# Early routing over 25 tiles with shorter last lags, and the next routing's compares behind the list in the experts

## The chip, the cores and the metric

The kernel runs on one core of a Trainium2 chip. The metric is the device time of one launch in microseconds (us); the times given are medians over runs. Engines are named as in the profile: PE is TensorE's matmul, PEld its weight load, DVE is VectorE, ACT is ScalarE, POOL is GpSimd, SP is SyncE, which issues most of the transfers.

## What is computed

Attention over 8 batches and 8 heads (S = 576 positions, D = 64), whose output, 4608 tokens of 512 numbers, goes through a mixture of 8 experts. Each token is given to one expert, each expert takes at most 576 tokens, and the pairs are handed out in the order of all logits from the largest down.

```python
def _attn_ref(q, k, v):                       # factor = 4, scale = 1 / sqrt(D)
    q_d = q.reshape(B, H, Sd, factor, D).mean(axis=3)      # k_d, v_d likewise
    out_up = np.repeat(sm_attn(q_d, k_d, v_d), factor, axis=2)
    mask = np.abs(pos[:, None] - pos[None, :]) < factor
    scores = np.where(mask, scale * np.matmul(q, k.transpose(0, 1, 3, 2)), -1000000000.0)
    ...
    return out_up + np.matmul(softmax(scores), v)

def _moe_ref(x, w_gate, w1, w2):
    logits = x @ w_gate                       # 4608 x 8
    order = np.argsort(-logits.flatten())
    for idx in order:
        tok, e = int(idx) // E, int(idx) % E
        if assigned[tok] >= 0 or counts[e] >= cap:         # cap = 576
            continue
        assigned[tok] = e
        counts[e] += 1
    for e in range(E):
        h = np.maximum(x[assigned == e] @ w1[e], 0.0)
        out[assigned == e] = h @ w2[e]
```

## The kernel before

**Attention.** The 4608 tokens are 36 tiles of 128 (index u), 4.5 to a batch. A tile goes through stages, each with a lag in the table LOC, counted in tiles: s0 and s1 (loc_s) make the scores of the band on PE, DVE takes their maximum (L541) and subtracts it (L542), ACT the exponential (L544); t (loc_t) transposes the result on PE (L552), and ACT copies it out as pt (L563); v0 and v1 (loc_v) multiply with v (L574), and norm divides by the sums on DVE (L450, L451, L453), which gives x. Then "add" (log_a) adds the downsampled attention's rows (L582, on POOL from the middle of the program), "st" stores x, "lt" (log_t) transposes x on PE (L592), ACT makes the high half of xt (L601) and DVE the low half (L602), and "lm" (log_m) makes the logits: four products with the high half (L617), four with the low half (L620), and a sum on DVE (L622) into lg.

The downsampled attention of a batch (down: scores, transposes of sd at L391 and L396, products with vd at L407 to L420) lies between these, spread from tile time DWS[b][0] to DWS[b][1] after the batch's first tile (DW where a batch has no entry). The transposes of q and k (L327) lie there too.

The order is written by hand: each step has a time in tiles (u + its lag), all steps are sorted by it, and each engine runs its instructions in that order. PE's steps are counted as pieces; "after(n, f)" puts f behind the n-th piece that follows, so FT is how many pieces behind the transposes the low half stands. From tile UE on, lags over 2 are shortened by the share CE for each tile. VWT is how far ahead of a tile its v is loaded. The loads and stores are issued by SP in the same order.

**Routing.** A logit becomes a key of two 16-bit halves, xh and xl (setup, L930 to L990). A search over the threshold that 576 tokens reach compares the keys with 64 thresholds at a time (compare, L822, into level[0] and level[1]) and counts the ones on PE (count, L855); three levels follow one another for xh and three for xl. Then rank (L909, L910) numbers the chosen tokens, the list turns the numbers into an index: ohh and ohl are one-hot rows of the high and low bits (L1099, L1112), r holds the rows of tokens (L1102, L1106), 18 products (L1115) add them up, and idx goes to the gathers. The counts, the rank, the list and the "sums" of totals (L898) share two PSUM buffers named pR in turn. The logits, setup and first level of tiles that are done are taken care of during attention: SETUP = {27: 0, 35: 28} starts setup over tiles 0 to 27 behind the logits of tile 27, and over 28 to 35 behind those of tile 35; SPACE is the distance of its steps in tiles. "ready" and "rest" prepare and finish the tables.

**Experts.** One expert after another: 576 tokens in 5 chunks, 312 products of xt with w1 (pH, L1258) and of ht with w2 (pX, L1299), each split into high and low halves. While expert i runs, the routing for expert i + 1 runs on DVE with its small products put between the big ones on PE: in the first stage after the products that TURN and BEHIND name, later by "place", which puts each group of routing products behind the last product whose planned time in the stage is not later than its entry in PACE (PACES for one stage). The last two of its 17 entries are those of the list and the sums. On DVE the instructions stand as the scheduler places them by their estimated times; a NoSync dependency ("behind_") makes one stand behind another.

## Time and profile before

| | |
|---|---|
| median of 3 runs | 720.87 us (719.96 to 724.84) |
| the profiled execution's own time | 722.95 us |
| its span | 721.3 us |
| mean granted clock of PE | 0.959 |
| PE busy | 648.9 us, 90% |
| DVE busy | 543.9 us, 75% |
| ACT busy | 338.2 us, 47% |
| POOL busy | 233.2 us, 32% |

The span is what the profile's times count from; the execution's own time has 1.65 us around it. The shares are means over pieces of different kind: attention until about 258 us, the last logits and the first routing until 298 us, eight experts of about 51 us each behind it. So the rows below are taken by stretches. In the rows "start, us" are the start and duration in microseconds; "out<-in" are the program's names without their numbers; the brackets at the end hold how long the engine had stood idle just before, and what it waited for.

### The profile page before, as it was taken

Reading aid. Unit: us, or ns where it says so; the run is one execution under the profiler, and the core shown is the slowest. Engines: PE = TensorE matmul, PEld = TensorE weight load, DVE = VectorE, ACT = ScalarE, POOL = GpSimd, SP = SyncE. Lnnn points to the kernel's source line nnn. Section 1 sums busy time; section 2 is a strip of 40 time slices with the busy share of each in tenths; the row PEclk is TensorE's granted clock in tenths of the full one; section 3 lists DMA queues with packets and bytes.
Section 4 is the critical chain, followed back from the end, with each engine's and each line's share of the span. In section 5 each row is a group of like instructions: output and inputs, shape, how many; then the busy total and the mean of one; then the engine's idle time right before and its main releaser. Section 6 shows DMA issues by size and latency. Waiting matters only on the chain.

```text
span 721.3 us, 21912 instructions
## 1 busy us (share of the span) xinstructions
PE 648.9 (90%) x8895; PEld 447.8 (62%) x8895; DVE 543.9 (75%) x1599; ACT 338.2 (47%) x649; POOL 233.2 (32%) x305
## 2 busy tenths in 40 slices
PE   7788999989899942899999899999999999999994
PEld 4566778777777731575575475574674674765841
DVE  5688989988989887887899698797797886533500
ACT  4448777787786520542442443443343324434410
POOL 4773565635737240401502402203103106202011
PEclk9799999999999965899999999999999999999997
DMA  9956779687985631704506817627647359806001
GB/s 261 230 149 192 223 191 232 191 216 197 230 220 155 177 112 48 251 2 166 200 1 252 172 25 265 151 82 231 120 149 195 90 202 212 317 21 111 2 30 37
DMA packets 132156, 113.71 MB, mean 158 GB/s; under 512 B 81240, under 2 KB 109912, under 8 KB 132056
## 3 DMA queue, kind: packets, MB, share of 16 engines
q1 hardware_dynamic: 124760, 90.76, 45.2%
q0 software_dynamic: 6432, 20.98, 9.5%
q8 instruction: 70, 1.15, 0.7%
q10 hardware_dynamic: 864, 0.58, 0.3%
q14 instruction: 30, 0.25, 0.1%
HBM read 85.74 MB, written 19.46 MB: 146 GB/s over the span
## 4 chain that ended last, share of the span: by engine, by line
PE 29%; DVE 20%; issue 15%; POOL 4%; DMA 3%; ACT 2%; POOLq 0%; SPq 0%; DVEq 0%; ACTq 0%
PE pX L1299 11%; PE pH L1258 10%; DVE level L822 2%; DVE wl L1182 2%; DVE ht L1285 2%; POOL xg L1197 2%; PE pR L855 2%; POOL out_dram L1309 2%; DMA xg<-x_dram,idx 1%; DVE x L453 1%; DVE ohl L1112 1%; PE g L574 1%; DVE cmp L822 1%; DMA nat<-in_moe_w_dram 1%; PE g L592 1%
## 5 line engine op out<-in xcount | busy, mean ns | idle before, releaser
L1258 PE MATMUL pH<-xt,wh 128*128 128x256 f16 (+1 forms) x1024 | 193.0, 286 | 2.3 <-ACT xt L1218 1.0
L1299 PE MATMUL pX<-wh,ht 128*128 128x512 f16 (+1 forms) x640 | 177.2, 379 | 0.0
L1258 PE MATMUL pH<-xt,wl 128*128 128x320 f16 (+1 forms) x512 | 146.1, 286 | 0.0
L1299 PEld LDWEIGHTS <-ht 128*128 128x128 f16 (+1 forms) x960 | 82.6, 100 | 95.1 <-issue 4.6
L1299 PE MATMUL pX<-wl,ht 128*128 128x512 f16 (+1 forms) x320 | 117.6, 379 | 0.0
L1258 PEld LDWEIGHTS <-wh 128*128 128x128 f16 x1024 | 97.4, 98 | 29.6 <-issue 5.2
L1309 POOL DMA_INDIRECT out_dram<-y,idx x40 | 42.7, 1067 | 177.7 <-ACT y L1306 155.0
L1182 DVE SCALAR_TENSOR_TENSOR wl<-nat,wh 128x512 f16<-128x512 f32 x128 | 83.3, 689 | 21.4 <-ACT wh L1180 18.7
L1282 ACT ACTIVATE ht<-pH 128x512 f16<-128x512 f32 (+1 forms) x128 | 45.5, 407 | 111.5 <-PE pH L1258 107.3
L1285 DVE SCALAR_TENSOR_TENSOR ht<-pH,ht 128x512 f16<-128x512 f32 (+1 forms) x128 | 52.2, 448 | 27.0 <-ACT ht L1282 26.4
L1306 ACT ACTIVATE y<-pX 128x512 f32<-128x512 f32 (+1 forms) x40 | 23.8, 594 | 102.3 <-issue 52.8
L1180 ACT ACTIVATE wh<-nat 128x1024 f16<-128x1024 f32 x64 | 67.4, 1053 | 9.1 <-DMA nat<-in_moe_w_dram 9.1
L1197 POOL DMA_INDIRECT xg<-x_dram,idx x40 | 42.3, 1057 | 67.6 <-DVE cl L1082 47.3
L1258 PEld LDWEIGHTS <-wl 128*128 128x128 f16 x512 | 49.9, 98 | 13.6 <-issue 1.8
L563 ACT COPY pt<-g 64x512 f32<-64x512 f32 x72 | 41.7, 580 | 34.9 <-PE g L552 33.9
L574 PE MATMUL g<-vw,pt 128*64 128x65 f32 x1152 | 45.1, 228 | 6.5 <-ACT pt L563 2.0
L574 PEld LDWEIGHTS g<-vw,pt 128*64 128x64 f32 x1152 | 39.1, 140 | 13.6 <-ACT pt L563 4.5
L327 PE MATMUL g<-ident,nat 128*128 128x128 f32 x256 | 41.0, 286 | 4.9 <-DMA nat<-in_q_dram 2.6
L313 ACT COPY kt<-g 64x512 f32<-64x512 f32 (+1 forms) x60 | 38.2, 636 | 7.6 <-PE g L327 6.4
L1005 POOL MEMSET f<- 128x1 bf16 x8 | 0.9, 110 | 118.5 <-DVE sumf L906 44.6
L1226 DVE SCALAR_TENSOR_TENSOR xs<-xg,xs 128x512 f16<-128x512 f32 (+1 forms) x30 | 20.4, 689 | 24.7 <-ACT xs L1225 18.6
L300 POOL TENSOR_TENSOR gtmp<-kt 128x576 f32<-128x576 f32 x14 | 16.0, 1146 | 64.7 <-ACT kt L313 54.0
(225 smaller groups left out, 1159.3 us busy)
## 6 DMA issues: line engine op xcount, KB each, us to landing
nat<-in_moe_w_dram SPq DMA_DIRECT2D x28, 1024.0 KB
vw<-in_v_dram SPq DMA_DIRECT2D x136, 78.0 KB
x_dram<-x SPq DMA_DIRECT2D x36, 256.0 KB
nat<-in_q_dram SPq DMA_DIRECT2D x32, 256.0 KB
nat<-in_k_dram SPq DMA_DIRECT2D x32, 256.0 KB
nat<-in_v_dram SPq DMA_DIRECT2D x28, 256.0 KB
up<-up_dram SPq DMA_DIRECT2D x9, 256.0 KB
nat<-in_moe_w_dram SPq DMA_DIRECT2D x4, 512.0 KB
```

What stands on the lines that cost most here:

```text
L313: self.nc.scalar.copy(out, in_)
L327: nc.tensor.transpose(p[:, a, :, fp], src[:, 4 * hh + 2 * a + s, 2 * fp:2 * fp + 2].rearrange("p f d -> p (f d)"), self.ident)
L563: self.nc.scalar.copy(out, in_)
L574: nc.tensor.matmul(o[64 * i:64 * i + 64, 65 * h:65 * h + 65], pt[:, 2 * (h % 2) + i, 2 * g + h // 2].rearrange("p b q -> p (b q)"), self.v ...
L1180: nc.scalar.activation(hi, r, AF.Copy, scale=sc)
L1182: nc.vector.scalar_tensor_tensor(lo[:, a:a + LOP], r[:, a:a + LOP], sc, hi[:, a:a + LOP], op0=OP.mult, op1=OP.subtract)
L1197: self.fetched = nc.gpsimd.indirect_dma_start(out=xg[:n], out_offset=None, in_=self.x, in_offset=bass.IndirectOffsetOnAxis(ap=idx[:n, c:c ...
L1258: mm = nc.tensor.matmul(p[:, s, :s1 - s0], w[d][a][:, 128 * f:128 * f + 128], xt[:, b, d, s0:s1], start=j == 0, stop=j == len(seq) - 1)
L1282: last = nc.scalar.activation(hi, q, AF.Relu)
L1285: low = nc.vector.scalar_tensor_tensor(lo, q, 0.0, hi, op0=OP.max, op1=OP.subtract)
L1299: mm = nc.tensor.matmul(p[o:o + m], ht[:, f, h0:h0 + m], w[4 + f // 2][b][:, 512 * (f % 2):512 * (f % 2) + 512], start=j < parts, stop=j > ...
L1309: i = nc.gpsimd.indirect_dma_start(out=self.out, in_=y[:n], in_offset=None, out_offset=bass.IndirectOffsetOnAxis(ap=idx[:n, c:c + 1], axis=0))
```

## The change

Two parts. The first changes numbers of attention's order, which move steps: the first batch's downsampled attention is stretched, the logits' lag goes up by a quarter of a tile and the transposes' lag of x goes down, early setup takes 25 tiles behind tile 24's logits (the last one 11), its steps lie wider apart, and the last lags are shortened from tile 33 on. The second makes the two first compares of the next routing stand behind the last operations of the current list on DVE (self.listed), and moves the places of list and sums on PE.

```diff
-FT = 4
+FT = 3
...
-DWS = {0: (1.96, 3.4), 7: (0.82, 2.25)}
-LOC = {'up': 2.07, 'um': 4.42, 'st': 4.6, 't': 1.194, 'lm': 8.07, ..., 'lt': 5.483, ...}
+DWS = {0: (1.95, 3.56), 7: (0.89, 2.3)}
+LOC = {'up': 2.07, 'um': 4.42, 'st': 4.6, 't': 1.194, 'lm': 8.317, ..., 'lt': 5.433, ...}
...
-SETUP = {27:0, 35:28}
-SPACE = 0.15
+SETUP = {24: 0, 35: 25}
+SPACE = 0.365
...
-VWT = 1.24
+VWT = 1.219
...
-UE = 35
-CE = 0.18
+UE = 33
+CE = 0.14
...
     def first_compare(self, i, key):
-        self.compare(self.level[i], key, self.first, 0, NT)
+        cmp = self.compare(self.level[i], key, self.first, 0, NT)
+        for ins in self.listed:
+            self.behind_(cmp, ins)
         return self.level[i]
...
-            nc.vector.tensor_scalar(r[:, :, 1], ohh, self.pcol, None, op0=OP.mult)
+            row = nc.vector.tensor_scalar(r[:, :, 1], ohh, self.pcol, None, op0=OP.mult)
...
-            nc.vector.tensor_tensor(ohl[:, a:b], pl[:, a:b, None].to_broadcast([128, b - a, 32]),
+            last = nc.vector.tensor_tensor(ohl[:, a:b], pl[:, a:b, None].to_broadcast([128, b - a, 32]),
...
+        self.listed = [last] if first and RACT else [last, row]
...
-BEHIND = ((1, 6), (2, 10))
+BEHIND = ((1, 6), (2, 2))
...
-PACE = (0, 4, 10.5, ..., 45.4, 46.2)
-PACES = {2: (0, 4.4, 10.5, 14.9, 17.3, 18.9, 20.4, 21, 23, 25, 27.3, 30, ..., 45.4, 46.2)}
+PACE = (0.6, 4, 10.5, ..., 43.9, 43)
+PACES = {2: (0.6, 4, 10.5, 13.9, 16.2, 18, 19.5, 20.4, 22.5, 24.8, 27, 30, ..., 43.9, 43)}
```

The first place is PE in the first batch, behind the scores (s) of one of its tiles; g are PSUM tiles, sd and sdt the downsampled scores, vw and pt the operands of the products with v. Before:

```order
L532 MATMUL s<-kt,qt 32x38 x32
L391 MATMUL g<-ident,sd 128x128 x9
L396 MATMUL g<-ident,sdt 128x128 x2
L574 MATMUL g<-vw_140,pt_146 64x65 x16
L407 MATMUL g<-vd_128,ptd 64x260 x2
L412 MATMUL g<-vd_128,ptd 64x65 x8
L552 MATMUL g<-ident,sw_143 128x128 x4
```

After:

```order
L532 MATMUL s<-kt,qt 32x38 x32
L391 MATMUL g<-ident,sd 128x128 x6
L574 MATMUL g<-vw_140,pt_146 64x65 x16
L391 MATMUL g<-ident,sd 128x128 x3
L396 MATMUL g<-ident,sdt 128x128 x2
L552 MATMUL g<-ident,sw_143 128x128 x4
L407 MATMUL g<-vd_128,ptd 64x260 x2
L412 MATMUL g<-vd_128,ptd 64x65 x8
```

A group of 16 products with v now stands between the second and the third three of sd's transposes. In all tiles the eight logit products (L617, L620) have gone from ahead of the transposes L552 to behind them (and behind a group of L327, where one stands there), ahead of the next tile's scores (L523, L532).

The second place is DVE at the end of attention, from the first compare of xl (level_83) to the last logits; lg are logits, xt low halves, den and x the normalization. Before:

```order
L450 TENSOR_SCALAR den<-g 128x4
L451 RECIPROCAL den<-den 128x4
L453 TENSOR_TENSOR x<-g,den 128x256
L822 TENSOR_TENSOR level_83<-xl,first 128x1152
L822 TENSOR_TENSOR level_83<-xl,first 128x640
L622 TENSOR_REDUCE lg<-g 128x8
L602 SCALAR_TENSOR_TENSOR xt<-g,xt 128x512
L622 TENSOR_REDUCE lg<-g 128x8 x2
L602 SCALAR_TENSOR_TENSOR xt<-g,xt 128x512
L622 TENSOR_REDUCE lg<-g 128x8
L602 SCALAR_TENSOR_TENSOR xt<-g,xt 128x512
```

After:

```order
L822 TENSOR_TENSOR level_83<-xl,first 128x1152
L450 TENSOR_SCALAR den<-g 128x4
L451 RECIPROCAL den<-den 128x4
L453 TENSOR_TENSOR x<-g,den 128x256
L450 TENSOR_SCALAR den<-g 128x4
L451 RECIPROCAL den<-den 128x4
L453 TENSOR_TENSOR x<-g,den 128x256
L602 SCALAR_TENSOR_TENSOR xt<-g,xt 128x512
L822 TENSOR_TENSOR level_83<-xl,first 128x448
L622 TENSOR_REDUCE lg<-g 128x8 x2
L602 SCALAR_TENSOR_TENSOR xt<-g,xt 128x512
L622 TENSOR_REDUCE lg<-g 128x8
```

The first piece of the compare of xl has gone from behind the last normalization to ahead of the last tile's two, and the second piece is 448 wide, not 640. Behind the last normalization five low halves and seven sums of logits stand in both orders. On POOL, four additions of x stand behind the copies of xl in the new order, three in the old.

The third place is DVE in the middle of an expert's second half: ohh, r and ohl belong to the list, level_82 and level_83 to the next routing, ht to the expert, n to the routing's rest. Line numbers after the change are higher by 2 or 3. Before:

```order
L1099 TENSOR_TENSOR ohh<-ph,io 128x648
L822 TENSOR_TENSOR level_82<-xh,first 128x2304
L1285 SCALAR_TENSOR_TENSOR ht<-pH,ht 128x512
L1285 SCALAR_TENSOR_TENSOR ht<-pH,ht 128x64
L822 TENSOR_TENSOR level_83<-xl,first 128x2304
L1102 TENSOR_TENSOR r<-ohh,t_5884 128x36x18
L1285 SCALAR_TENSOR_TENSOR ht<-pH,ht 128x512
L1285 SCALAR_TENSOR_TENSOR ht<-pH,ht 128x64
L1106 TENSOR_SCALAR r<-ohh,tabs 128x36x18
L1112 TENSOR_TENSOR ohl<-pl,io 128x1152
L1074 SCALAR_TENSOR_TENSOR n_8083<-pR,n_8083 128x36
```

After:

```order
L1101 TENSOR_TENSOR ohh<-ph,io 128x648
L1114 TENSOR_TENSOR ohl<-pl,io 128x1152
L1288 SCALAR_TENSOR_TENSOR ht<-pH,ht 128x512
L1288 SCALAR_TENSOR_TENSOR ht<-pH,ht 128x64
L1104 TENSOR_TENSOR r<-ohh,t_5884 128x36x18
L1108 TENSOR_SCALAR r<-ohh,tabs 128x36x18
L822 TENSOR_TENSOR level_82<-xh,first 128x2304
L1288 SCALAR_TENSOR_TENSOR ht<-pH,ht 128x512
L1288 SCALAR_TENSOR_TENSOR ht<-pH,ht 128x64
L822 TENSOR_TENSOR level_83<-xl,first 128x2304
L1123 COPY odd<-pR 32x36
L1076 SCALAR_TENSOR_TENSOR n_8083<-pR,n_8083 128x36
```

The two compares have gone behind the list's operations; n, which reads the rank, stands behind all of them as before. On PE, the number of big products of a stage ahead of a routing group is now, in the three middle stages: list 201 (208 before), sums 206 (212), first level 219 (216). In the first stage the list stands at 243 (251), in the second at 214 (225), its sums at 226 (225) and its first level at 231 (233); in the last stage with a routing the list is at 201 (208), and the sums too (212).

## Rows read from the trace of the kernel before

**Rows 1.** Windows: stretch, length, busy of PE PEld DVE ACT POOL, PEclk, DMA, GB/s

```profile
35.00:40.00 5.00, 3.57 (x47) 3.03 (x49) 4.86 (x18) 2.46 (x8) 4.17 (x7) 0.72 0.87 224
200.00:240.00 40.00, 37.94 (x1011) 30.89 (x1010) 34.29 (x98) 27.97 (x59) 19.99 (x26) 1.00 0.66 181
240.00:260.00 20.00, 14.38 (x423) 12.08 (x395) 17.75 (x52) 9.30 (x17) 7.66 (x12) 0.98 0.55 169
266.50:297.70 31.20, 13.24 (x131) 8.43 (x131) 24.05 (x99) 6.84 (x9) 5.67 (x10) 0.57 0.32 100
297.70:722.00 424.30, 404.25 (x3149) 252.74 (x3148) 297.26 (x897) 155.82 (x291) 81.86 (x84) 0.99 0.45 135
```

**Rows 2.** Waits of PE up to 258: us in total, times, longest

```profile
PE g L552 <- ACT sw L544: 4.8, 8, 1.1
...
PE g L574 <- ACT pt L563: 2.0, 3, 0.9
```

**Rows 3.** Waits of PE in the experts, from 297

```profile
PE pR L1115 <- DVE ohl L1112: 2.6, 4, 1.0
```

**Rows 4.** Timeline of PE in the first batch: start, us, instruction

```profile
36.43 0.55 PE L391 MATMUL g<-ident,sd 128*128 128x128 f32 x3 [1.84 <-ACT sd L375]
...
43.72 1.16 PE L574 MATMUL g<-vw,pt 128*64 128x65 f32 x32
```

**Rows 5.** Timeline of DVE in the first batch

```profile
43.09 0.16 DVE L450 TENSOR_SCALAR den<-g 128x5 f32<-128x5 f32 x1 [1.43 <-PE g L420]
```

**Rows 6.** Timeline of PE at the end of attention

```profile
254.61 0.24 PE L617 MATMUL g<-wg,xt 128*128 128x16 f16 x4
254.71 0.24 PE L620 MATMUL g<-wg,xt 128*128 128x8 f16 x4
...
258.72 0.86 PE L592 MATMUL g<-ident,x 128*128 128x128 f32 x4 [2.61 <-POOL x L582]
```

**Rows 7.** Timeline of DVE at the end of attention

```profile
250.38 1.16 DVE L948 TENSOR_TENSOR s<-s,m 128x28 int32<-128x28 int32 x1
251.58 0.18 DVE L953 TENSOR_SCALAR h<-s 128x28 int32<-128x28 int32 x1
...
255.07 1.15 DVE L822 TENSOR_TENSOR level<-xh,first 128x1152 bf16<-128x1152 int16 x2
...
257.36 0.42 DVE L453 TENSOR_TENSOR x<-g,den 128x256 f32<-128x256 f32 x1
257.70 3.05 DVE L822 TENSOR_TENSOR level<-xl,first 128x1152 bf16<-128x1152 int16 x2
...
265.23 0.17 DVE L622 TENSOR_REDUCE lg<-g 128x8 f32<-128x16 f32 x1 [0.37 <-PE g L620]
265.32 0.68 DVE L602 SCALAR_TENSOR_TENSOR xt<-g,xt 128x512 f16<-128x512 f32 x1
266.36 0.17 DVE L622 TENSOR_REDUCE lg<-g 128x8 f32<-128x16 f32 x1 [0.36 <-PE g L620]
```

**Rows 8.** Timeline of POOL at the end of attention

```profile
250.23 1.27 POOL L582 TENSOR_TENSOR x<-x,up 128x512 f32<-128x512 f32 x1
...
257.40 4.47 POOL L582 TENSOR_TENSOR x<-x,up 128x512 f32<-128x512 f32 x3
```

**Rows 9.** Timeline of ACT at the end of attention

```profile
263.90 0.60 ACT L601 ACTIVATE xt<-g 128x512 f16<-128x512 f32 x1 [0.55 <-PE g L592]
```

**Rows 10.** Timeline of DVE in the fourth expert's stage, at the list

```profile
487.12 1.34 DVE L822 TENSOR_TENSOR level<-xh,first 128x2304 bf16<-128x2304 int16 x1
...
491.82 1.34 DVE L1112 TENSOR_TENSOR ohl<-pl,io 128x1152 bf16<-128x1152 int16 x1
493.09 0.18 DVE L1074 SCALAR_TENSOR_TENSOR n<-pR,n 128x36 f32<-128x36 f32 x1
```

**Rows 11.** Timeline of PE in the same stage

```profile
493.22 0.76 PE L1115 MATMUL pR<-r,ohl 128*128 128x72 bf16 x18 [0.69 <-DVE ohl L1112]
...
494.68 0.17 PE L898 MATMUL pR<-sums,one 128*128 128x8 bf16 x1
```

More of the change, by code (lines that the diff above doesn't have):

```diff
@@ L52 @@
 DW = (0.15, 1.9)
-DWS = {0: (1.96, 3.4), 7: (0.82, 2.25)}
-LOC = {'up': 2.07, 'um': 4.42, 'st': 4.6, 't': 1.194, 'lm': 8.07, 's0': 0.33, 's1': 0.331, 'lt': 5.483, 'v0': 1.842, 'v1': 1.843, 'add': 4.425}
+DWS = {0: (1.95, 3.56), 7: (0.89, 2.3)}
+LOC = {'up': 2.07, 'um': 4.42, 'st': 4.6, 't': 1.194, 'lm': 8.317, 's0': 0.33, 's1': 0.331, 'lt': 5.433, 'v0': 1.842, 'v1': 1.843, 'add': 4.425}
 GS1 = ''
@@ L1111, in emit @@
         for a, b in EH if first else WHOLE:
-            nc.vector.tensor_tensor(ohl[:, a:b], pl[:, a:b, None].to_broadcast([128, b - a, 32]),
-                                    self.io[:, None, :32].to_broadcast([128, b - a, 32]), op=OP.is_equal)
+            last = nc.vector.tensor_tensor(ohl[:, a:b], pl[:, a:b, None].to_broadcast([128, b - a, 32]),
+                                           self.io[:, None, :32].to_broadcast([128, b - a, 32]), op=OP.is_equal)
             for t in range(a, b, 2):
@@ L1328 @@
 LEAD = -19.0
-PACE = (0, 4, 10.5, 13, 15.3, 17, 18.5, 19.2, 21.5, 24, 26.5, 30, 32.5, 36.5, 37.2, 45.4, 46.2)
-PACES = {2: (0, 4.4, 10.5, 14.9, 17.3, 18.9, 20.4, 21, 23, 25, 27.3, 30, 32.5, 36.5, 37.2, 45.4, 46.2)}
+PACE = (0.6, 4, 10.5, 13, 15.3, 17, 18.5, 19.2, 21.5, 24, 26.5, 30, 32.5, 36.5, 37.2, 43.9, 43)
+PACES = {2: (0.6, 4, 10.5, 13.9, 16.2, 18, 19.5, 20.4, 22.5, 24.8, 27, 30, 32.5, 36.5, 37.2, 43.9, 43)}
 SPIN = 24
```

## The prediction

> **What bounds the kernel now.** I read the sum of each engine by stretches of the span first [rows 1]. From 200 to 240 us TensorE works 37.94 of 40 us, VectorE 34.29: the middle of the attention is bound by TensorE, and only what makes TensorE wait costs time. From 240 to 260 it works 14.38 of 20, and VectorE 17.75: here the attention runs out and the bound goes over to VectorE. From the last logit at 266.5 to the first expert product at 297.7 TensorE works 13.24 of 31.2; this is the first routing, a chain of small steps that cannot begin before the last logit. After it TensorE works 404.25 of 424.3 us and its products follow one another. So the time is four pieces in a row. Whatever brings the last logit forward moves all that follows by as much; in the experts only a wait of TensorE counts.
>
> Then I read what TensorE waits for. Up to 258 us the transposes of the local scores (L552) wait 4.8 us in 8 places for the exponentials, and the products with v (L574) 2.0 us in 3 places [rows 2]. In the experts the list's products (L1115) wait 2.6 us in 4 places for VectorE's comparison with the low bits [rows 3]; that is all that part B can remove there.
>
> **Part A, first batch.** The new times of the downsampled attention put one group of 16 products with v into the middle of the transposes of sd (L391), where TensorE stood 1.84 us for ScalarE's exponentials [rows 4]. Two such groups take 1.16 us at full clock [rows 4], and they come out of a place where nothing waited, so up to 1.2 us is saved. Against it stands that VectorE is busy 4.86 of the 5 us from 35 to 40 [rows 1]; if it sets the pace there, nothing is saved. It isn't busy throughout: at 43.09 it had stood 1.43 us for TensorE [rows 5]. At most the whole stall goes, and with it the lower clock: 0.72 was granted in those 5 us [rows 1], between the levels 1.2 and 2.4 GHz, which is 5 x 0.28 = 1.4 us of work. Bounds 0 and -3.2; I take **-1.2**.
>
> **Part A, logits behind the transposes.** In every tile the logit products (L617, L620) move from ahead of loc_t to behind it. Two sets of four take 0.24 us each and start 0.10 apart [rows 6], about 0.35 us. Before, they gave the exponentials 0.35 us more before TensorE asked for them. In the 8 tiles in which TensorE waits there anyway [rows 2] the wait now grows: 8 x 0.35 = +2.8. Behind the transposes they give as much to the copies of pt, on which L574 waits in 3 places [rows 2]: -3 x 0.35 = -1.0. Elsewhere TensorE has 0.35 us less ahead of one wait and more ahead of another, and nothing is lost. I take the middle, **+0.9**, bounds -1.0 and +2.8.
>
> **Part A, up to the last normalization (L453).** The early routing setup now takes 25 tiles and is spread wider, so its steps stand some three tiles sooner on VectorE and POOL. Before, this stretch was where VectorE ran full: of 20 us it had 2.25 us left [rows 1]. Two costs show. L948, on 28 numbers, took 1.16 us from 250.38, as long as POOL's addition of 1.27 us from 250.23 [rows 7, 8]; L953 behind it, on as many numbers, took 0.18 [rows 7], so about 1.0 us went to the neighbour. It now stands among other work, and I count it as gained. Half of the 2.25 us that VectorE stood should come back too, 1.1 us, as the steps are spread. Against this the first compare of xl, which stood behind the last normalization, now stands ahead of it: 1152 columns take some 0.75 us of the 1.15 that 1792 columns of xh took [rows 7], and up to 1.0 with a neighbour. -1.0 - 1.1 + 1.0 = **-1.1**. The bounds: all of the idle time and L948's against a compare at 0.75 (-2.5), or nothing gained and two more such meetings at 1.0 each (+2.0).
>
> By the Trainium skill, "SBUF — State Buffer", section "Who interferes with whom", VectorE and GpSimd share a pair of ports as an exclusive lock: a VectorE instruction with two SBUF inputs contends with a GpSimd instruction that reads SBUF, and whoever starts first holds it for the whole instruction. L948's row agrees, with 1.16 us beside POOL's 1.27. The rule speaks against this change as well: the two compares of xl still stand among POOL's last additions, and with two meetings of 1.27 us the sum below would be 2.5 smaller, about 719 in place of the value that I give.
>
> **Part A, from the last normalization to the last logit.** Before it took 266.36 + 0.17 - (257.36 + 0.42) = 8.75 us [rows 7]. The rows show why: the compares of xl took 3.05 us there, for what took 1.15 with xh, and POOL's last three additions 4.47 beside them instead of 3 x 1.27 [rows 7, 8]; TensorE stood 2.61 us for the first of them [rows 6]; then the tiles went through at 1.13 us each (265.23 to 266.36 [rows 7]), since the low half of a tile (L602) waits for its high half on ScalarE. In the new order 448 columns of one compare are left behind the last normalization. What has to come after it in any order is one chain: an addition 1.27, four transposes 0.86, the high half 0.60, the low half 0.68, logit products 0.35, a sum 0.17 [rows 6 to 9] = 3.9 us. But five low halves stand behind it in both orders; at 1.13 each that is 5.7, and with the addition ahead of them and the 448 columns (0.4) it is 7.4. I take the middle, 5.65, so **-3.1**, bounds -4.85 and -1.35.
>
> **Part A, the last setup** takes 11 tiles, not 8. A compare of 28 tiles took 1.15 [rows 7], 0.04 us a tile; three tiles more in each of two compares make **+0.2**. The other changed numbers of part A (the low half one piece sooner, the loads of v 0.02 of a tile sooner on SP's queue, last lags shortened from tile 33 on) add and remove no instruction; what they move is in the two terms above, and the stores of x, which stand behind the additions on SP, go forward with these.
>
> **Part B.** In the three middle stages the wait at the list goes. In the third of them ohl (1.34) ended at 493.16 and TensorE's list started at 493.22, after 0.69 us of waiting; two compares of 1.34 stood ahead of it [rows 10, 11]. Now they stand behind, and the list's place is 7 products sooner (208 to 201), some 1.5 us, which VectorE's 2.7 us cover: no wait is left at the list. But the sums (L898) use the buffer of the rank, which is free when n (L1074) has read it, and n now stands behind both compares. n stood at 493.09 [rows 10] and stays there within 0.2 us, since the same operations stand ahead of it in another order. The sums, at 494.68 with the wait in it [rows 11], move 6 products forward: 494.68 - 0.69 - 6 x 0.22 = 492.7, so they wait 0.6 to 0.8 us. The wait moves from list to sums; nothing is gained or lost. In the second routing the list stands 11 products sooner and in the first of the stages 8; one wait goes and the first level count meets a later compare. All of it **-0.2**, bounds -2.6 (all four waits gone [rows 3]) and +1.0. The gathers start 1.2 us sooner, but their products are an expert away.
>
> **Sum.** -1.2 + 0.9 - 1.1 - 3.1 + 0.2 - 0.2 = -4.5. The profiled execution took 722.95 us, its span 721.3; 722.95 - 4.5 = 718.45. It stood 2.08 above the median of the runs, 720.87, so the median after is **716.4 us**, a gain of 0.6%. What a measurement of this kernel can tell from no change is about 1%, 7.2 us.
>
> **Rivals.** First, *the compares still meet POOL's last additions*. For it: four additions and 1600 columns of xl stand together in the new order too, and 3.05 in place of 1.15 shows the price. Against: the larger compare stands a tile sooner. Then the tail stays 8.7 and the end of the normalizations at +1.0 in place of -1.1; the sum is -1.2 + 0.9 + 1.0 + 0.2 - 0.2 = +0.7 at worst, about 0 when the first meeting hides: 720.9 us. Chance 0.24.
>
> Second, on the other side, *the logits lengthen the loop of every tile*. If scores, maximum, exponentials, transposes is the chain that sets the pace of a tile, 0.35 us more ahead of the next scores cost 36 x 0.35 = 12.6 us in place of 0.9: 728.1 us. It decides from 15 tiles on, where 5.4 us of the other terms are used up. Against: TensorE works 95% of 200 to 240 us and waits at L552 in 8 tiles only [rows 1, 2]. Chance 0.06.
>
> Third, *the list's waits really go*, because the sums find their buffer free (n between the compares, or a rank read sooner): 2.4 us more, 714.0 us; a tail at its bare chain of 3.9 gives about the same by itself. Chance 0.15.
>
> **How the numbers follow.** My forecast has 0.55; by its terms' bounds, of which not all fall on one side, its own range is 713.5 to 719. The range for 8 in 10 takes in the first rival with a part of what is worse, and the third: 711.5 to 722. Faster by over 1% means below 713.7: half of the third rival and a tenth of the forecast, 0.13. Slower by over 1% is above 728.1: half of the second rival and a little, 0.04. Within 1%: 0.83.
>
> **What would show it.** Right: the last normalization ends near 256.4 (257.78 - 1.2 + 0.9 - 1.1) and the last logit 5 to 6 us behind it; the compares of xl take under 2 us together; no wait at L1115 in the middle stages but one of 0.5 to 1 at L898; a few more waits at L552. The wait at 36.43 in sd shrinks to under 0.8. Wrong would make it: compares of xl that again take 3 us, waits at L552 in more than 15 tiles, or a sum at L898 that does not wait.

## The result and the profile after

| | before | after |
|---|---|---|
| median of 8 runs each, in turn on one chip | 723.81 us (719.96 to 725.72) | 716.45 us (711.64 to 718.06) |
| ratio, 95% interval | | 0.990 (0.9875 to 0.9926) |
| the profiled execution's own time | 722.95 us | 718.0 us |
| its span | 721.3 us | 716.3 us |

The prediction was 716.4 us with a range of 711.5 to 722.0, and it named a change within 1% as the likeliest; the ratio measured, 0.990, lies at the edge of that. The median before, taken beside the changed kernel, stood 2.9 us above the one that the prediction started from, so the gain by medians is 7.4 us (5.4 to 9.0 by the interval of the ratio). Between the two profiled executions it is 5.0 us of span, against the 4.5 us of the sum. In a later comparison (the changed kernel beside the one with the compares behind n, below) the ratio was 0.9933 (0.9903 to 0.9962), a gain of 4.9 us (4.2 by the medians).

Where the 5.0 us lie is read from landmarks of the two traces. The maximum of a tile is L541 on VectorE, counted from the first; the last normalization, the last logit and the first expert product are those of the prediction.

| landmark | before | after | difference |
|---|---|---|---|
| maximum of the 4th tile starts | 44.57 | 41.42 | -3.15 |
| maximum of the 5th tile starts | 52.66 | 49.90 | -2.76 |
| maximum of the 35th tile starts | 244.12 | 243.24 | -0.88 |
| last normalization ends | 257.78 | 254.99 | -2.79 |
| last logit ends | 266.53 | 260.34 | -6.19 |
| first expert product starts | 297.77 | 291.85 | -5.92 |
| end of the span | 721.3 | 716.3 | -5.0 |

The fourth tile's maximum has also moved in the order: its scores (L523, L532) now stand ahead of the last 52 products with vd on TensorE, and the maximum itself ahead of the last normalization of the downsampled attention on VectorE. By the fifth tile's maximum VectorE has run the same operations in both kernels, so 2.8 us is the lead that counts.

The end of attention, VectorE's timeline of the changed kernel, from the first piece of the compare of xl on (columns as in [rows 7], which holds the same lines of before):

```profile
251.82 1.70 DVE L822 TENSOR_TENSOR level<-xl,first 128x1152 bf16<-128x1152 int16 x1
...
254.57 0.42 DVE L453 TENSOR_TENSOR x<-g,den 128x256 f32<-128x256 f32 x1
254.91 0.68 DVE L602 SCALAR_TENSOR_TENSOR xt<-g,xt 128x512 f16<-128x512 f32 x1
255.51 0.83 DVE L822 TENSOR_TENSOR level<-xl,first 128x448 bf16<-128x448 int16 x1
...
257.12 1.28 DVE L602 SCALAR_TENSOR_TENSOR xt<-g,xt 128x512 f16<-128x512 f32 x2
...
259.11 0.69 DVE L602 SCALAR_TENSOR_TENSOR xt<-g,xt 128x512 f16<-128x512 f32 x1 [0.24 <-ACT xt L601]
...
260.17 0.17 DVE L622 TENSOR_REDUCE lg<-g 128x8 f32<-128x16 f32 x1 [0.29 <-PE g L620]
```

One compare now stands ahead of the last normalizations, a small one behind them, and two low halves follow one another without a pause at 257.12, where before a sum of logits that had waited some 0.4 us for TensorE stood between any two [rows 7]. In the experts the waits of TensorE changed places. From 290 us on, in the changed kernel (in us, times, longest):

```profile
PE pR L900 <- DVE n L1076: 3.2, 3, 1.3
```

The list's row of before, 2.6 us in 4 places [rows 3], is gone; a row of 3.2 us in 3 places at the sums (L900, L898 in before) has come. The timelines of VectorE and then TensorE in the fourth expert's stage, to be set beside [rows 10, 11]:

```profile
482.13 1.34 DVE L1114 TENSOR_TENSOR ohl<-pl,io 128x1152 bf16<-128x1152 int16 x1
...
484.83 1.34 DVE L822 TENSOR_TENSOR level<-xh,first 128x2304 bf16<-128x2304 int16 x1
...
486.83 1.33 DVE L822 TENSOR_TENSOR level<-xl,first 128x2304 bf16<-128x2304 int16 x1
...
488.20 0.18 DVE L1123 COPY odd<-pR 32x36 f32<-32x36 f32 x1
488.42 0.20 DVE L1076 SCALAR_TENSOR_TENSOR n<-pR,n 128x36 f32<-128x36 f32 x1
```

```profile
485.86 0.75 PE L1117 MATMUL pR<-r,ohl 128*128 128x72 bf16 x18
...
488.67 0.18 PE L900 MATMUL pR<-sums,one 128*128 128x8 bf16 x1 [0.98 <-DVE n L1076]
```

ohl ends at 483.47, the list starts without a wait, and the sums start when n has read the rank, 0.05 us behind its end at 488.62.

### The profile page after: what moved, and what is told of

Read it like the earlier page. It is cut to its first block, busy times and chain, and to the rows that moved or that the text cites. A ratio compares the mean times of both kernels' runs of the same rounds, so it can differ in the third digit from the quotient of the medians.

```text
span 716.3 us, 21890 instructions
## 1 busy us (share of the span) xinstructions
PE 646.5 (90%) x8895; PEld 447.9 (63%) x8895; DVE 539.8 (75%) x1599; ACT 337.5 (47%) x649; POOL 232.2 (32%) x305
## 4 chain that ended last, share of the span: by engine, by line
PE 36%; DVE 24%; issue 18%; DMA 10%; ACT 6%; POOL 3%; SPq 1%; POOLq 0%; ACTq 0%; DVEq 0%
PE pX L1302 10%; PE pH L1261 9%; PE g L327 2%; DVE wl L1185 2%; DMA vw<-in_v_dram 2%; DVE ht L1288 2%; PE g L574 2%; DVE level L822 2%; PE pR L857 2%; POOL out_dram L1312 2%; PE g L552 2%; DMA xg<-x_dram,idx 2%; PE s L532 1%; DMA nat<-in_moe_w_dram 1%; DVE x L453 1%
## 5 line engine op out<-in xcount | busy, mean ns | idle before, releaser
L1185 DVE SCALAR_TENSOR_TENSOR wl<-nat,wh 128x512 f16<-128x512 f32 x128 | 83.4, 687 | 17.1 <-ACT wh L1183 14.8
L574 PE MATMUL g<-vw,pt 128*64 128x65 f32 x1152 | 44.3, 226 | 5.8 <-issue 2.7
L574 PEld LDWEIGHTS g<-vw,pt 128*64 128x64 f32 x1152 | 38.5, 138 | 12.8 <-issue 6.1
L327 PE MATMUL g<-ident,nat 128*128 128x128 f32 x256 | 41.0, 286 | 3.5 <-DMA nat<-in_q_dram 1.9
```

What stands on the lines that cost most here:

```text
L327: nc.tensor.transpose(p[:, a, :, fp], src[:, 4 * hh + 2 * a + s, 2 * fp:2 * fp + 2].rearrange("p f d -> p (f d)"), self.ident)
L574: nc.tensor.matmul(o[64 * i:64 * i + 64, 65 * h:65 * h + 65], pt[:, 2 * (h % 2) + i, 2 * g + h // 2].rearrange("p b q -> p (b q)"), self.v ...
L1185: nc.vector.scalar_tensor_tensor(lo[:, a:a + LOP], r[:, a:a + LOP], sc, hi[:, a:a + LOP], op0=OP.mult, op1=OP.subtract)
```

## Experiments

Theory 1, as it stood after the comparison of the traces: the gain is made before the last logit, in the first batch (a stall is filled and TensorE keeps its upper clock) and at the end of attention (setup out of the way); part B moves a wait from the list to the sums and gains nothing. The rivals stand with each run. A ratio is that to the kernel before, in runs on the same chip, with a 95% interval.

**One part alone.** Part A, with `first_compare`, BEHIND, PACE and PACES as before:

```diff
-        for ins in self.listed:
-            self.behind_(cmp, ins)
...
-BEHIND = ((1, 6), (2, 2))
+BEHIND = ((1, 6), (2, 10))
```

> Part A alone: attention's new order numbers, with the list and the compares in the experts as before. Theory 1 (the gain is made before the last logit, part B costs): the last logit comes at about 260.3 us as in the changed kernel, the waits at the list are back with some 2.6 us, none of 1.0 at the sums, and the stretch from the last logit to the end is that of before, 454.8 us, so the time is about 1 us below the changed kernel's: ratio to before about 0.989. Rival (part B gains in the experts): the time is 2 to 3 us above the changed kernel's, ratio about 0.993.

Measured: 0.9915 (0.9894 to 0.9936), last logit at 256.91 us, the list's waits back with 2.6 us in 4 places, none at the sums. Part B, with the numbers of attention as before:

> Part B alone: the compares behind the list and the new places of list and sums, with attention's order as before. Theory 1: the last logit stays at 266.5 us, the list no longer waits, the sums wait about 1 us in each of three stages, and the time is that of before or up to 1.2 us more: ratio 1.000 to 1.002. Rival (part B gains): 2 to 3 us less, ratio about 0.996.

Measured: 1.0013 (0.999 to 1.0037), last logit at 267.58 us, 3.2 us in 3 places at the sums. So part A carries the whole gain (whether it is faster alone than the changed kernel, 0.990 and 0.9933, can't be told), and part B changes nothing that these runs can tell: the interval allows a gain of 0.7 us or a loss of 2.7.

**What the sums wait for.** The changed kernel, with the two compares behind n too:

```diff
-                nc.vector.scalar_tensor_tensor(n1, rk[:, 1], float(CAP - OUT), n1, op0=OP.is_lt, op1=OP.add)
+                self.listed.append(nc.vector.scalar_tensor_tensor(n1, rk[:, 1], float(CAP - OUT), n1, op0=OP.is_lt, op1=OP.add))
```

> The changed kernel, with the two compares behind n as well (the step that reads the rank and so frees the buffer that the sums need). Theory 1 (the sums wait for that buffer and for nothing else): the waits of 1.3, 1.0 and 1.0 us at the sums go, the list waits no more either, and the time falls by about 3 us against the changed kernel, to a ratio of about 0.986. Rival (the sums then wait for something behind it, or the level count meets its compare later): the same waits turn up at the level count or at the sums' own reduction, and the time stays within 1 us.

Measured: the row at L900 is gone, as the timelines of the second execution (below) show, VectorE first:

```profile
482.86 1.34 DVE L1114 TENSOR_TENSOR ohl<-pl,io 128x1152 bf16<-128x1152 int16 x1
485.56 0.18 DVE L1076 SCALAR_TENSOR_TENSOR n<-pR,n 128x36 f32<-128x36 f32 x1
485.67 1.34 DVE L822 TENSOR_TENSOR level<-xh,first 128x2304 bf16<-128x2304 int16 x1
```

```profile
486.60 0.75 PE L1117 MATMUL pR<-r,ohl 128*128 128x72 bf16 x18
487.18 0.17 PE L900 MATMUL pR<-sums,one 128*128 128x8 bf16 x1
```

n stands ahead of the compares, and the sums follow the list without a wait, although they now stand 5 big products sooner on TensorE (201 of a stage ahead of them, not 206) and so ask for the buffer earlier. From the first product to the end it took 422.0 us, against 424.45 in the changed kernel's profile. But the ratio was 0.9904 (0.9873 to 0.9934), that of the changed kernel. Since medians of different sets were compared there, it was run again beside the changed kernel itself:

> The changed kernel itself, on the same chip as the next three, so that these can be set against it. Theory 1 and the rival alike: ratio to before 0.990.

> The changed kernel with the two compares behind n as well, a second time. Its experts took 422.0 us in the profile against 424.45 of the changed kernel, but its ratio to before was the same. Theory 1 (the waits at the sums are time of the whole): 2 to 2.5 us less than the changed kernel, ratio 0.987. Rival (what the experts gain there is lost elsewhere, or the profile's difference is one of executions): within 1 us of the changed kernel, 0.990.

Measured: the changed kernel 722.08 us, 0.9933 (0.9903 to 0.9962), experts 425.83 us; with the compares behind n 718.56 us, 0.9882 (0.9842 to 0.9922), experts 422.96 us. The two profile pairs agree on 2.5 and 2.9 us less in the experts, and the medians of this group on 3.5 us less. The intervals of the two ratios still overlap, so the size stays rough; that the waits of 3.2 us at the sums are those for the rank's buffer is shown.

What these waits are worth in time is not settled. Two runs further down (the old place of the logits in tiles 0 to 23, without and with setup's steps closer together) have the same instructions in the same order on each engine in the experts, and no row at L900 for n either, but their experts took 425.3 and 425.5 us. TensorE's waits for the routing's flag had grown, from 1.1 and 1.0 us in 2 places to 2.9 and 5.2 in 4. The longest of them, 2.61 us, in the run with the closer steps, TensorE, VectorE and ScalarE:

```profile
455.42 0.17 PE L875 MATMUL pR<-flag,one 128*128 128x8 bf16 x1 [2.61 <-DVE flag L870]
```

```profile
454.50 0.68 DVE L1229 SCALAR_TENSOR_TENSOR xs<-xg,xs 64x512 f16<-64x512 f32 x1 [1.53 <-ACT xs L1228]
455.21 0.15 DVE L870 TENSOR_TENSOR flag<-pR,less 32x8 bf16<-32x8 f32 x1
```

```profile
453.84 0.63 ACT L1228 ACTIVATE xs<-xg 64x512 f16<-64x512 f32 x1 [2.29 <-DMA xg<-x_dram,idx]
```

The flag stands behind a conversion of gathered tokens on VectorE, and ScalarE had stood 2.29 us for these tokens; in the second execution with the compares behind n the flag in this place came without a wait of TensorE. So a late gather can cost the experts as much as the reordering gives.

**What the first batch is worth.** The changed kernel with `DWS = {0: (1.96, 3.4), 7: (0.82, 2.25)}` of before, which takes back the last batch's two numbers together with the first one's:

> The changed kernel with the downsampled attention of the first and the last batch at its old times. Theory 1 (the first batch gave 3.1 us by the fourth tile, of which the stall at the transposes of sd and the lower clock behind it are the cause): the fourth tile's maximum comes at about 44.5 us and not 41.4, the wait of 1.8 us at the third group of sd's transposes is back, and what of it is left at the last logit, with the later waits that eat part of it, is 1 to 3 us. Rival (the gain there is eaten by later waits in any case): the first batch is 3 us later, but the last logit within 0.5 us of the changed kernel's 260.3.

Measured: 0.9979 (0.995 to 1.0007). The fourth tile's maximum is at 44.97 us, the stall of sd's transposes at 1.94 us, and the last logit at 262.11 us, where five executions with the changed attention had it at 256.7 to 260.9. So a part of the first batch's gain reaches the last logit; what the last batch's numbers do is not separated here. The other way round, the kernel before with the first batch's two numbers and nothing else:

```diff
-DWS = {0: (1.96, 3.4), 7: (0.82, 2.25)}
+DWS = {0: (1.95, 3.56), 7: (0.82, 2.25)}
```

> The kernel before with nothing but the first batch's new times, DWS[0] = (1.95, 3.56). Theory 1 (the group of products with v that now stands in the stall of sd's transposes is all that is needed, and it keeps TensorE at its upper clock): the granted clock from 36 to 42 us is 1.00, where before shows 0.79, 0.50 and 0.85 in three stretches of 2 us; the fourth tile's maximum comes at 40.4 to 41.4 us in place of 44.6, and the time falls by 3 to 4 us, ratio 0.995. Rival (the gain needs the other numbers, the low half that stands a piece sooner among them): the fourth tile's maximum is at 43 us or later and the ratio above 0.998.

Measured: 0.9956 (0.9928 to 0.9983), so 3.2 us (1.2 to 5.2) by two numbers, as theory 1 has it. The fourth tile's maximum is at 40.85, and of its lead of 3.7 us 3.1 are there at the 19th tile, 2.6 at the 31st and 2.4 at the last logit. What TensorE did shows in windows of 2 us (columns as in [rows 1]; the clock is the third number from the end). Before:

```profile
36.00:38.00 2.00, 1.57 (x21) 1.40 (x23) 1.97 (x6) 1.94 (x7) 1.84 (x3) 0.79 0.76 184
38.00:40.00 2.00, 2.00 (x32) 1.62 (x30) 1.93 (x11) 0.00 (x0) 1.85 (x5) 0.50 0.96 263
40.00:42.00 2.00, 2.00 (x32) 1.61 (x31) 1.46 (x7) 0.58 (x1) 1.84 (x4) 0.85 0.84 196
```

The first batch's numbers alone:

```profile
36.00:38.00 2.00, 1.83 (x27) 1.36 (x25) 2.00 (x6) 1.55 (x6) 1.84 (x3) 1.00 0.91 225
38.00:40.00 2.00, 2.00 (x94) 1.67 (x96) 1.86 (x12) 1.16 (x2) 1.85 (x6) 1.00 0.68 199
40.00:42.00 2.00, 1.96 (x64) 1.62 (x61) 1.86 (x8) 0.00 (x0) 1.84 (x3) 1.00 0.37 74
```

Before, TensorE is busy throughout from 38 to 42 us and yet slow: the granted clock is down to 0.50, the 1.2 GHz level, and the same four products of vd take 1.09 us in before and 0.66 in the changed kernel:

```profile
38.90 1.09 PE L407 MATMUL g<-vd,ptd 128*64 128x260 f32 x4
```

```profile
38.36 0.66 PE L407 MATMUL g<-vd,ptd 128*64 128x260 f32 x4
```

With the new numbers the granted clock from 38 to 42 us is 1.00 in all eleven executions; with the old ones it is 0.50 to 0.85 in three, each behind a stall of 1.84 to 1.96 us. From the third tile's scores to the first scores of the next batch (L356 at 44.80 before, 43.32 in the changed kernel) TensorE has the same products in both orders and takes 12.14 us before, 10.42 in the changed kernel and 10.41 with the two numbers alone. Its waits in this stretch fell from 1.84 us to 1.46 and 1.41, so about 1.3 of the 1.7 us are the clock's. The changed kernel's own lines in that place:

```profile
35.48 0.55 PE L391 MATMUL g<-ident,sd 128*128 128x128 f32 x3 [1.27 <-ACT sd L375]
35.95 1.15 PE L574 MATMUL g<-vw,pt 128*64 128x65 f32 x32
37.04 0.55 PE L391 MATMUL g<-ident,sd 128*128 128x128 f32 x3
```

The stall itself only shrank from 1.84 us [rows 4] to 1.27; the products stand behind the second three of the transposes, not in the stall ahead of them.

But TensorE does not set the pace here. VectorE is busy 1.9 of 2 us in most of these windows, and from the third tile's maximum to the fifth's it has the same 42 operations in every kernel: 16.88 to 16.92 us in the three executions with the old numbers, 13.96 to 14.66 in the eleven with the new. Before, it stood 1.43 us for the last products with vd (L420) [rows 5], which TensorE's stall and lower clock made late; this wait of 1.43 to 1.67 us is gone in ten of the eleven and 0.58 in one. In the changed kernel these products start 1.1 us sooner (41.23 against 42.36), and VectorE does the fourth tile's maximum and subtraction, 0.9 us, ahead of what needs them. The other part is a meeting of VectorE with POOL. Before, VectorE and then POOL:

```profile
45.57 2.14 DVE L471 SCALAR_TENSOR_TENSOR u<-xu,u 64x512 f16<-64x512 f32 x2
47.74 0.95 DVE L471 SCALAR_TENSOR_TENSOR yh<-yu,yh 128x64 f16<-128x64 f32 x1
```

```profile
45.70 1.46 POOL L279 TENSOR_TENSOR vd<-gtv,identb 128x512 f32<-128x512 f32 x1
...
47.27 1.34 POOL L473 TENSOR_TENSOR ut<-yh,identb 128x512 f16<-128x512 f16 x1
```

In the changed kernel the same operations of VectorE come ahead of these two of POOL:

```profile
44.12 1.55 DVE L471 SCALAR_TENSOR_TENSOR u<-xu,u 64x512 f16<-64x512 f32 x2
45.70 0.23 DVE L471 SCALAR_TENSOR_TENSOR yh<-yu,yh 128x64 f16<-128x64 f32 x1
```

The three took 3.06 us in each execution with the old numbers and 1.75 in each with the new, 1.3 less. The wait of 1.4 and these 1.3 make up, but for 0.3 us, what VectorE gains between the third and the fifth maximum, 2.6 us in the changed kernel and 3.0 with the two numbers alone.

**The logits behind the transposes.** The changed kernel with lags lm 8.07 and lt 5.483 in all tiles, and, with the compares behind n, in tiles 0 to 23 alone:

```diff
-                at = u + lag
+                at = u + (lag := OLD.get(name, lag) if u < 24 else lag)     # OLD = {'lm': 8.07, 'lt': 5.483}
```

> The changed kernel with the logit products ahead of loc_t again (lags lm 8.07 and lt 5.483). Theory 1 (behind the transposes they cost: of the first batch's 3.1 us some 2 are lost again by the 25th tile, where the transposes wait 8.2 us for the exponentials and not 4.8): the waits at L552 are near 5 us again, the 25th tile's maximum comes 2.5 to 3 us sooner than in before, and the time is 1.5 to 2 us below the changed kernel's, ratio 0.9875. Rival (those waits are places where tiles wait for transfers or VectorE in any case): the same tile times as the changed kernel within 0.5 us, ratio 0.990.

> The changed kernel with the two compares behind n, and the old lags of the logits (lm 8.07, lt 5.483) for tiles 0 to 23, the new ones behind them. Theory 1 (behind the transposes the logits cost in the loop, with 0.3 to 0.7 us more in each of some five waits at L552, and gain 2.3 us in the tail, so that each place is right in one part of attention): the waits at L552 up to 240 us are near 6.5 us or less, the tail stays at 5.2 us, and the time is 1 to 2 us below that of the kernel with the compares behind n alone, ratio 0.986. Rival (the longer waits at L552 only take the place of others): the tail is 5.2 us and the time within 1 us of that kernel's, ratio 0.9885.

Measured: all tiles 0.9916 (0.9884 to 0.9948), tiles 0 to 23 0.994 (0.9907 to 0.9973). TensorE's waits from 45 to 240 us, the row for L552 of before, of the changed kernel and of the old lags in tiles 0 to 23:

```profile
PE g L552 <- ACT sw L544: 4.6, 7, 1.1
...
PE g L574 <- ACT pt L563: 1.1, 2, 0.6
```

```profile
PE g L552 <- ACT sw L544: 8.2, 8, 2.1
...
PE g L574 <- ACT pt L563: 2.0, 4, 0.6
```

```profile
PE g L552 <- ACT sw L544: 6.0, 7, 1.4
```

So a part of the longer wait at L552 belongs to the logits' place (7.0 to 8.3 us in eight executions with the new place, 5.4 to 6.5 in three with the old one, 4.6 to 5.2 in the kernel before, with part B alone and with the first batch's numbers alone). The time does not tell whether it costs anything. The old place in all tiles took 2.0 us less than the changed kernel by the medians of the same set (720.12 against 722.08), as theory 1 has it, but the intervals of the two ratios overlap in most of their length; the mix of both places was no faster than the new place in all tiles, and its ratio of 0.994 (its medians stand at 0.992) meets neither theory 1 nor the rival. From the 4th tile's maximum to the 35th's, five executions of one and the same order took 200.3 to 202.9 us, and those with the old place 200.35 and 200.7 (203.35 with setup's steps closer together), within that spread or near it; before took 199.55, and part B alone, with the same attention, 200.7. That the waits cost time in the loop isn't shown. What the place does show is the tail from the last normalization to the last logit: 7.58 us with the old lags in all tiles, 4.9 to 5.35 with the new ones, and 5.06 where only the last tiles have them.

**What shortens the end.** Setup as before (`SETUP = {27:0, 35:28}`, `SPACE = 0.15`), and the last lags as before (`UE = 35`, `CE = 0.18`, `FT = 4`), each in the changed kernel:

> The changed kernel with early setup over 28 tiles and its steps close together (SETUP and SPACE of before); the last lags stay shortened. Theory 1 (the compares of xl that meet POOL's last additions behind the last normalization make the tail): the two compares of xl take 3 us again, the last normalization comes 1 to 2 us later, the tail to the last logit is 8 to 9 us in place of 5.35, and the time is 4 to 5 us above the changed kernel's, ratio 0.996. Rival (the shortened last lags and the low half that stands a piece sooner make the tail): the tail stays under 6.5 us and the time within 2 us of the changed kernel's, ratio 0.992.

> The changed kernel with the last lags and the place of the low half as before (UE 35, CE 0.18, FT 4). From the last but one tile's maximum to the last logit before takes 22.1 us, the changed kernel 15.5 to 17.1; with the old setup it took 19.4, with the old place of the logits 18.15. Theory 1 (setup and the logits' place make most of it, and what is left for the last lags is the rest, some 0.8 us): 16.5 to 17.5 us, a tail of 5.5 to 6.5 us, and a ratio within 0.002 of the changed kernel's 0.990 to 0.993. Rival (the last lags are needed for either to show): 18.5 us or more, ratio 0.996.

Measured: 0.994 (0.9912 to 0.9967) and 0.9921 (0.9893 to 0.9949). With the old setup the tail took 7.35 us, between the 8 to 9 of theory 1 and the 6.5 of the rival; with the old lags the two stretches took 17.7 us, just above the 17.5 of theory 1, and the tail 6.10, within its bounds. The end of attention repeats within 1.6 us from one execution to the next, and so it tells more than the ratios:

| us | 35th maximum to last normalization | to the last logit | both |
|---|---|---|---|
| attention as before (3 executions) | 13.1 to 13.7 | 8.75 | 21.8 to 22.4 |
| changed (5 executions) | 10.6 to 11.75 | 4.9 to 5.35 | 15.5 to 17.1 |
| old setup | 12.07 | 7.35 | 19.4 |
| old place of the logits | 10.57 | 7.58 | 18.15 |
| old last lags | 11.57 | 6.10 | 17.7 |
| old place of the logits in tiles 0 to 23 | 10.91 | 5.06 | 16.0 |
| the same, setup's steps closer together | 11.62 | 4.36 | 16.0 |

Against the middle of the changed executions, 16.2, the old setup costs 3.2 us, the old place of the logits 1.9 and the old lags 1.5; together 6.6, of 5.9 that the whole is worth. Each of these is one execution against a spread of 1.6 us, so the setup's share is clear, the logits' place likely, and that of the lags, 0.6 us above the slowest of the five, the least sure.

**The neighbours.** The kernel with the compares behind n and the old lags in tiles 0 to 23 once more, with `SPACE = 0.2`, so that no compare is left behind the last normalization:

> The same with the early setup's steps closer together (SPACE 0.2 in place of 0.365), so that no compare stands behind the last normalization. Theory 1 (a compare beside one of POOL's additions is held for as long as that addition takes: 1152 columns took 1.70 us and 448 took 0.83 there, 1600 columns of xh without that neighbour 1.05): the compares of xl take under 1.5 us together where POOL's additions don't lie beside them, and the last normalization comes 0.5 to 1.5 us sooner counted from the last maximum; the time falls by 0.5 to 1 us more, ratio 0.985. Rival (the steps now stand among tiles at which VectorE is the bound, and hold back their maximum and normalization): the last maximum comes 1 to 2 us later and the time is that of the wider spacing or more, ratio 0.987 or above.

Measured: 0.9958 (0.9933 to 0.9983), the end of attention 16.0 us as with the wider spacing. The last normalization did not come sooner; what was taken from the tail was put ahead of it, and the 35th maximum came 2.6 us later than with the wider spacing, as the rival has it. The compares tell a part of why. With the closer spacing, VectorE, then POOL:

```profile
245.60 1.81 DVE L822 TENSOR_TENSOR level<-xl,first 128x1152 bf16<-128x1152 int16 x1
...
249.41 0.38 DVE L822 TENSOR_TENSOR level<-xl,first 128x448 bf16<-128x448 int16 x1
```

```profile
245.53 1.27 POOL L582 TENSOR_TENSOR x<-x,up 128x512 f32<-128x512 f32 x1
...
249.70 1.26 POOL L582 TENSOR_TENSOR x<-x,up 128x512 f32<-128x512 f32 x1 [0.92 <-DMA up<-up_dram]
```

With the wider one (the run with old lags in tiles 0 to 23):

```profile
250.44 0.75 DVE L822 TENSOR_TENSOR level<-xl,first 128x1152 bf16<-128x1152 int16 x1
```

```profile
250.73 1.59 POOL L582 TENSOR_TENSOR x<-x,up 128x512 f32<-128x512 f32 x1 [0.63 <-issue]
```

The compare that begins 0.07 us behind an addition takes 1.81 us, about 1.06 more than the 0.75 of the one that begins 0.29 us ahead of an addition; there the addition takes 1.59 in place of 1.27. In both pairs the one that starts second is held.

## Why the prediction held, point by point

**First batch.** Right in direction, too small in size, and the mechanism only in part. The step took -1.2 out of bounds of 0 and -3.2; by the fifth maximum the lead was 2.8 us, and the two numbers alone are worth 3.2 us by the ratio. The 1.2 were to be products that fill TensorE's stall, but the stall shrank by 0.6 and its sign (under 0.8 us) failed with 1.27; TensorE's gain was mostly the clock, which the step had worked out (1.4 us) and left at the bound. What counts is VectorE, which sets the pace: its wait of 1.43 us, which the step read and used only as an argument, is the most that TensorE's gain could give at that place, and the 1.3 us of its meeting with POOL stand in no term. That the bound of -3.2, built from TensorE's stall and clock, lies near the measured lead is chance. One line was read with a wrong count: the x32 of [rows 4] is one group of 16 products, each of which leaves two records, not two groups; the price of 1.2 is that of the group that moved.

**Logits behind the transposes.** The growth of the wait at L552 was forecast as 2.8 us and is 2.4 to 3.6 in five executions, of which the old place takes back some 1 to 2. The credit of 1.0 at L574 did not come: from 45 to 240 us its row went from 1.1 us to 2.0 in the changed kernel's profile, and to 1.1 to 1.7 in four other executions. What the step missed is the other side of the edit: it shortens the tail by about 2 us, which the sum had put down to setup alone. Whether the +0.9 is right can't be told, since the same order repeats only within 2.6 us over those tiles. The second rival's 12.6 us did not come: from the 4th tile's maximum to the 35th's the time grew by 2.3 us.

**Up to the last normalization.** Forecast -1.1; the stretch from the 35th maximum went from 13.66 to 11.75 in the two profiles, -1.9, and by the middles of several executions about -2.4. The 1.0 of L948 came (L950 now, 0.17 us at 238.06). The other two terms did not come as put. The compare of xl met an addition and cost 1.70 in this profile, not 1.0; of VectorE's idle time there only 0.3 us came back (1.81 to 1.55), not 1.1. What the step left out is that with L948 the other steps of setup have left the stretch too. Before:

```profile
248.52 0.38 DVE L940 TENSOR_REDUCE m<-lg 128x28 f32<-128x224 f32 x1
...
249.03 0.55 DVE L946 TENSOR_TENSOR eq<-lg,m 128x224 bf16<-128x224 f32 x1
...
251.67 0.53 DVE L955 TENSOR_REDUCE am<-eq 128x28 f32<-128x224 bf16 x1
...
253.60 0.87 DVE L976 TENSOR_TENSOR oh<-eq,amu 128x224 bf16<-128x224 bf16 x1
```

With the 1.16 of L948 these are 3.5 us of VectorE's work, of which 0.26 is left in the changed kernel (L978, the old L976). VectorE's busy time in the stretch went from 11.85 to 10.21 us. The size came near by errors that cancel.

**The tail.** Forecast 5.65 us, measured 5.35, and 4.9 to 5.2 in four other executions: the middle between the bare chain and five low halves one by one came out, with two low halves at a time once. Of the 3.4 us, 2.2 are the compares of xl, 3.05 us there before and 0.83 now. The place of the logits, to which the step gave nothing here, has its part (7.58 us with the old one), so the value is better than its reason.

**Neighbours.** The Trainium skill's rule in "SBUF — State Buffer", section "Who interferes with whom", holds in both directions here: 1.70, 1.81 and 1.88 us for 1152 columns beside an addition (the last with the old lags) against 0.75 alone, and an addition of 1.59 against 1.27 where the compare came first. In the changed kernel's profile both compares met an addition, 1.70 and 0.83 us against 0.75 and 0.38, a price of 1.4 us; together they took 2.5, where the prediction's sign of being right was under 2 and that of being wrong 3. So the first rival's mechanism happened, but it did not undo the tail. That price was paid inside a sum that gained more elsewhere than was forecast, 1.3 us of it where such a meeting went away, at L471 in the first batch.

**Last setup.** Forecast +0.2; from the last logit to the first product 31.24 became 31.51 in the two profiles, +0.27.

**Part B.** Forecast -0.2, with the wait moving from the list to the sums. It moved as told; three waits of 1.3, 1.0 and 1.0 us stand at the sums, where 0.6 to 0.8 was worked out for one. In the stage of that working one instruction makes the difference: `odd`, which needs the list's result, now stands between the second compare and n and takes 0.2 us. The experts took 424.45 us in place of 423.53, +0.9, but not all of this is part B. The three middle stages took 0.4, 0.3 and 0.5 us more, 0.2 to 0.3 of it in each by the longer wait; the first stage took 1.5 us more, with TensorE's granted clock at 0.66 in its first 5 us against 1.00 before; and two other stages took 1.6 less together. The third rival, the waits really gone, is what the compares behind n give: the waits go, and 2.5 to 2.9 us with them in two executions out of four.

So the total of -4.5 came near the measured -5.0 of the two profiles with errors that cancel: some 2 us too little gain by the fourth tile and 1.1 too little at the end, against 1.4 too little cost from the 4th tile to the 35th (their time grew by 2.3 us between the profiles, of which a spread of 2.6 between equal executions may be all) and 1.1 in the experts. The range held. The agreement to 0.05 us with the median is chance, all the more as the median before had moved by 2.9 us.

## What to carry to other kernels

A stall of one engine is to be priced by what the engine that sets the pace gets from it. Here TensorE gained 1.7 us, 1.3 of them by its clock, but VectorE set the pace and got back at most the 1.4 us that it had waited. The next step is to look at which operations of VectorE and GpSimd lie side by side after the shift: another 1.3 us came from a meeting that went away. When a comparison is put behind other work on an in-order engine, look for the instruction that frees a buffer for someone else and put that ahead of it too: one line (n ahead of the compares) took away waits of 3.2 us, though a late gather can hide the gain. An edit whose cost in the steady loop could not be told apart from the spread seems to have gained about 2 us at the end of the loop, so ends and middles are to be costed apart.

## What the runs showed that was not expected

The wait for the first gather differs by about 2 us between executions of one and the same kernel. The first transposes of the gathered tokens, in the changed kernel's two profiles:

```profile
288.98 0.66 PE L1217 MATMUL pX<-ident,xg 128*128 128x128 f32 x4 [1.62 <-DMA xg<-x_dram,idx]
```

```profile
291.33 1.12 PE L1217 MATMUL pX<-ident,xg 128*128 128x128 f32 x4 [2.69 <-DMA xg<-x_dram,idx]
```

From the last logit they start 28.6 and 30.4 us later, and the whole stretch to the first product took 31.2 to 31.8 us in six executions and 33.1 to 33.8 in eight, with nothing between. The granted clock in the first 5 us of the experts differs as well: 1.00 in four of the six and 0.66 and 0.50 in the others, 0.50 to 0.71 in all of the eight; the first expert's stage takes 57.2 to 57.6 us at 1.00 and 59.0 to 59.5 at 0.50. All this and the middle of attention hide differences of 2 us and more between single profiles; the end of attention repeats to 1.6 us.

The granted clock of 0.50 lasted through windows in which TensorE was fully busy (38 to 40 us in before, and 38 to 42 at 0.56 and 0.59 in the run with the old first batch). A busy share of 2.00 of 2 there was work at half speed.
